# A decode-attention loop: the gather of a head's sums moved into the next pass, and half of a small projection moved ahead of the last gather

## Chip, cores and metric

The kernel runs on one core of a Trainium2 chip. The metric is the time of one execution in device microseconds (us). "Span" is the time from the first to the last instruction in the trace; it is about 1.7 us shorter than the time of the same run.

## The reference

Two independent blocks of attention for one new token, joined in the last dimension. Both have 32 query heads of 128, a query projection `x @ wq` and an output projection `@ wo` to 512 columns.

```
A: 32 heads, each with its own K and V of 32768 keys          (the large block)
B: 8 K/V heads shared by 4 query heads each, last 4096 keys   (the small block)

q = (x @ wq), per head;  p = softmax(q . K^T / sqrt(128));  o = p @ V
out = concat(o_A @ wo_A, o_B @ wo_B)                          all bf16
```

A head of the large block needs 8 MB of K and 8 MB of V. In all 570 MB have to come from HBM, and each byte is used once.

## The kernel before

The small block comes first. Then the TensorE (PE) and the VectorE (DVE) run a loop over the 32 heads of the large block; the loads are issued without a loop. The parts that matter (cuts marked with `...`, the comments are added here):

```python
        for g in range(NQH):
            self.loop = {"pe": g, "dve": g // 2}
            self.load_k(g, 1 if 0 < g < NQH - 1 else 2)   # K, the first and the last head's in two halves
            self.load_v(g)
            self.emit_qcopy(g)
            self.emit_unit("A", g)     # transpose K, score it (psT, kt, psS)
            self.emit_stats("A", g)    # maximum and exponentials
            self.emit_PT("A", g)
            self.emit_PV("A", g)       # V product (psACC), folds, gather
        self.loop = {}
        for n in ("B", "A"):
            for part in range(len(self.WO_CUTS[n]) - 1):
                self.load_wo(n, part)  # B in 2 pieces, A in 6 ever smaller ones
        self.emit_spread("A")
        self.emit_proj()               # small block's projection, then the large one's
```

The V product leaves four 4x128 blocks per strip in PSUM. The end of `emit_PV`:

```python
        pv = self.emit_gather(name, g, DH, DH + 1)      # the sum of exponentials
        ...
        for j in range(4):                              # four "folds" on the VectorE
            ...                                         # oc = block * one-hot (+ oc)
        self.accread = o
        self.gath = self.emit_gather(name, g, 0, DH)    # "gather": adds the head's row to psG
```

So at the end of each pass the TensorE waits for four folds, does one small product (the gather), goes back to the loop's top, and can then begin to transpose the next K. K sits in thirds of a buffer of which a head uses two; V has one buffer. The next K load is issued in the middle of a unit, the next V load when the V product is done.

## Time and profile before

| | before |
|---|---|
| time, median of the first 3 runs | 1323.44 us (1322.58 to 1323.79) |
| time, median of the 6 runs on record once the result was in (the same 3 and 3 more) | 1322.7 us (1322.35 to 1323.79) |
| span of the profiled run | 1321.7 us |
| distance of two 8 MB landings in the loop (K, V, K, ...) | 19.3 us throughout |
| last landing of projection weights | 1318.8 us |

First the page's slices. Each digit is the busy share of one fortieth of the span in tenths, or the TensorE clock granted in it:

```profile
PEclk9886788887878888787888878888887788888788
DMA  9999999999999999999999999999999999999998
```

The transfers are busy from end to end. The page's groups of instructions (busy time and mean ns of one, then the idle time before them and what ended most of it):

```profile
L557 DVE COPY kt<-psT 128x1024 bf16<-128x1024 bf16 x1056 | 654.3, 683 | 236.9 <-PE psT L553 235.5
L553 PE MATMUL psT<-ident,kbuf 128*128 128x128 bf16 x8448 | 577.8, 234 | 169.0 <-DMA kbuf<-in_A_k_cache_dram 154.4
```

The second line has the TensorE waiting 154.4 us for K. One boundary between passes in the timeline (start, length, engine, line and operation; in brackets the idle time before it and what ended it):

```profile
1234.97 0.33 SPq L326 DMA_DIRECT2D vbuf<-in_A_v_cache_dram  x1
...
1236.58 0.41 PE L683 MATMUL psG<-oc_A,hw 128*32 128x128 f32 x2 [1.63 <-DVE oc_A L672]
1241.26 5.15 PE L553 MATMUL psT<-ident,kbuf 128*128 128x128 bf16 x64 [4.27 <-DMA kbuf<-in_A_k_cache_dram]
```

The next V load is issued at 1234.97, the gather waits 1.63 us for the folds, and then 4.27 us pass until K has landed. So the queue always has the next load before the current one ends. Only the last boundary is different, because the last K comes in halves:

```profile
1274.41 0.41 PE L683 MATMUL psG<-oc_A,hw 128*32 128x128 f32 x2 [1.64 <-DVE oc_A L672]
...
1275.77 3.82 PE L553 MATMUL psT<-ident,kbuf 128*128 128x128 bf16 x64 [0.95 <-PEq L262]
```

Here K had landed, and 1.36 us lie between gather and transpose; 0.95 of them are put down to the TensorE's sequencer (PEq), which is the loop's back edge. The tail, from the last V product (L656) over the last gather (L683), the small block's projection (L733), the copy of its four strips (L736) and their sum (L737) to the large block's projection (L741, L719) and the store:

```profile
1284.84 2.70 SPq L326 DMA_DIRECT2D kbuf<-in_A_wo_dram  x6
...
1300.21 6.30 PE L656 MATMUL psACC<-vbuf,ptsb 128*4 128x512 bf16 x64 [0.69 <-ACT ptsb L631]
...
1308.19 0.41 PE L683 MATMUL psG<-oc_A,hw 128*32 128x128 f32 x2 [1.64 <-DVE oc_A L672]
...
1309.61 3.31 PE L733 MATMUL psS<-kbuf,oz_B 128*1 128x512 bf16 x32
...
1312.97 0.69 DVE L736 COPY pb<-psS 128x512 f32<-128x512 f32 x1 [3.07 <-PE psS L733]
...
1313.71 1.02 PE L737 MATMUL psACC<-pb,e 128*1 128x512 f32 x2 [0.80 <-DVE pb L736]
...
1314.57 2.10 PE L741 MATMUL psT<-kbuf,oz_A 128*1 128x512 bf16 x9
...
1319.09 0.93 PE L719 MATMUL psPT<-kbuf,oz_A 128*1 128x256 bf16 x14
...
1320.55 0.25 SPq L755 DMA_DIRECT2D out_dram<-out_sb  x1
```

The TensorE never waits for weights there. The last of the six loads, issued by 1287.1, took 31.7 us to land (the page's DMA issues), which gives the 1318.8 of the table.

### The profile page before, as it was taken

Reading aid. Unit: us, or ns where it says so; the run is one execution under the profiler, and the core shown is the slowest. Engines: PE = TensorE matmul, PEld = TensorE weight load, DVE = VectorE, ACT = ScalarE, POOL = GpSimd, SP = SyncE. Lnnn points to the kernel's source line nnn. Section 1 sums busy time; section 2 is a strip of 40 time slices with the busy share of each in tenths; the row PEclk is TensorE's granted clock in tenths of the full one; section 3 lists DMA queues with packets and bytes.
Section 4 is the critical chain, followed back from the end, with each engine's and each line's share of the span. In section 5 each row is a group of like instructions: output and inputs, shape, how many; then the busy total and the mean of one; then the engine's idle time right before and its main releaser. Section 6 shows DMA issues by size and latency. Waiting matters only on the chain. (4 is left out here: it accounts for less than half of the span.)

```text
span 1321.7 us, 28783 instructions
## 1 busy us (share of the span) xinstructions
PE 968.2 (73%) x13243; PEld 673.7 (51%) x13243; DVE 750.7 (57%) x1341; ACT 55.1 (4%) x168; POOL 2.6 (0%) x22
## 2 busy tenths in 40 slices
PE   4675768777677878767787777678777667877787
PEld 3353446555444655544465544446554445555453
DVE  3563556664555666455566645556665456665563
ACT  0000000000000000000000000000000000000000
POOL 0000000000000000000000000000000000000000
PEclk9886788887878888787888878888887788888788
DMA  9999999999999999999999999999999999999998
GB/s 404 434 434 431 440 434 434 434 436 432 433 436 436 428 438 434 428 438 434 428 442 430 428 442 432 430 438 434 437 432 432 438 430 434 438 428 436 436 428 365
DMA packets 13359, 570.59 MB, mean 432 GB/s; under 512 B 1570, under 2 KB 1700, under 8 KB 2084
## 3 DMA queue, kind: packets, MB, share of 16 engines
q1 hardware_dynamic: 13060, 570.43, 99.8%
q8 instruction: 8, 0.13, 0.0%
q10 hardware_dynamic: 288, 0.00, 0.0%
q14 instruction: 3, 0.02, 0.0%
HBM read 570.43 MB, written 0.00 MB: 432 GB/s over the span
## 5 line engine op out<-in xcount | busy, mean ns | idle before, releaser
L557 DVE COPY kt<-psT 128x1024 bf16<-128x1024 bf16 x1056 | 654.3, 683 | 236.9 <-PE psT L553 235.5
L553 PE MATMUL psT<-ident,kbuf 128*128 128x128 bf16 x8448 | 577.8, 234 | 169.0 <-DMA kbuf<-in_A_k_cache_dram 154.4
L553 PEld LDWEIGHTS psT<-ident,kbuf 128*128 128x128 bf16 x8448 | 538.1, 106 | 261.2 <-DMA kbuf<-in_A_k_cache_dram 162.5
L656 PE MATMUL psACC<-vbuf,ptsb 128*4 128x512 bf16 (+1 forms) x2112 | 187.0, 531 | 22.8 <-ACT ptsb L631 22.0
L576 PE MATMUL psS<-kt,qw 128*32 128x512 bf16 x2048 | 157.7, 385 | 14.9 <-DVE kt L557 14.9
L670 DVE TENSOR_SCALAR oc_A<-psACC,hot_A 128x128 f32<-128x128 f32 x32 | 11.2, 350 | 251.9 <-PE psG L683 251.9
L656 PEld LDWEIGHTS psACC<-vbuf,ptsb 128*4 128x4 bf16 (+1 forms) x2112 | 59.8, 111 | 140.4 <-issue 93.1
L604 ACT ACTIVATE psb<-psS,nb_A 128x512 bf16<-128x512 f32 x32 | 22.0, 687 | 1166.5 <-DVE nb_A L603 1166.5
L576 PEld LDWEIGHTS psS<-kt,qw 128*32 128x32 bf16 x2048 | 34.0, 95 | 57.6 <-DVE kt L557 30.8
L683 PE MATMUL psG<-oc_A,hw 128*32 128x128 f32 (+1 forms) x128 | 19.3, 227 | 52.3 <-DVE oc_A L672 52.3
L683 PEld LDWEIGHTS psG<-oc_A,hw 128*32 128x32 f32 x128 | 11.4, 109 | 62.4 <-DVE oc_A L672 55.0
L628 PE MATMUL psPT<-ident,psb 128*128 128x128 bf16 x136 | 18.3, 279 | 34.0 <-ACT psb L604 34.0
L672 DVE SCALAR_TENSOR_TENSOR oc_A<-psACC,hot_A,oc_A 128x128 f32<-128x128 f32 x96 | 33.6, 350 | 3.4
L593 DVE TENSOR_REDUCE tr_in<-psS 128x1 f32<-128x512 f32 x34 | 23.5, 692 | 17.2 <-PE psS L576 17.2
L628 PEld LDWEIGHTS psPT<-ident,psb 128*128 128x128 bf16 x136 | 10.3, 119 | 37.1 <-ACT psb L604 36.7
L597 PE MATMUL psACC<-rows,tr_in 128*1 128x64 f32 x64 | 8.7, 217 | 25.6 <-DVE tr_in L593 25.6
L631 ACT ACTIVATE ptsb<-psPT 128x512 bf16<-128x512 bf16 x34 | 20.3, 597 | 30.9 <-PE psPT L628 30.9
L597 PEld LDWEIGHTS psACC<-rows,tr_in 128*1 128x1 f32 x64 | 2.7, 81 | 35.1 <-DVE tr_in L593 35.1
L601 PE MATMUL psACC<-mr_A,nscale 1*128 1x1 f32 x64 | 12.1, 256 | 9.8 <-DVE mr_A L600 9.8
L601 PEld LDWEIGHTS psACC<-mr_A,nscale 1*128 1x128 f32 x64 | 9.4, 182 | 15.8 <-DVE mr_A L600 15.8
L603 DVE COPY nb_A<-psACC 128x1 f32<-128x1 f32 x32 | 5.0, 157 | 15.1 <-PE psACC L601 15.1
L600 DVE TENSOR_REDUCE mr_A<-psACC 1x1 f32<-1x64 f32 x32 | 6.8, 213 | 11.7 <-PE psACC L597 11.7
(82 smaller groups left out, 74.9 us busy)
## 6 DMA issues: line engine op xcount, KB each, us to landing
kbuf<-in_A_k_cache_dram SPq DMA_DIRECT2D x4, 4096.0 KB, 23.2
kbuf<-in_B_k_cache_dram SPq DMA_DIRECT2D x2, 4096.0 KB, 31.6
vbuf<-in_B_v_cache_dram SPq DMA_DIRECT2D x2, 4096.0 KB, 25.4
vbuf<-in_B_wq_dram SPq DMA_DIRECT2D x1, 4096.0 KB, 12.4
vbuf<-in_A_wq_dram SPq DMA_DIRECT2D x1, 4096.0 KB, 31.9
kbuf<-in_B_wo_dram SPq DMA_DIRECT2D x2, 2048.0 KB, 33.1
kbuf<-in_A_wo_dram SPq DMA_DIRECT2D x1, 1408.0 KB, 27.4
kbuf<-in_A_wo_dram SPq DMA_DIRECT2D x1, 1024.0 KB, 29.5
```

Source lines behind the costliest of these rows:

```text
L553: inst = e.transpose(T[:, 128 * k:128 * k + 128], src[:, DH * k:DH * k + DH], self.ident[:, :])
L557: self.copies.append(self.op("dve", lambda v: v.tensor_copy(KT[:, :], T[:, :]), o, to="pe"))
L576: inst = e.matmul(self.S[32 * c:32 * c + 32, :], lhsT=win, rhs=self.kt[(bb + c // 2) % NKT][:, 512 * (c % 2):512 * (c % 2) + 512], start=b ...
L593: o = dve(lambda v: v.reduce_max(tr["in"][:, 0:1], self.S[:, :], axis=AXX), self.sdone, self.k_pool, to="pe" if name == "A" else None)
L597: o = self.op("pe", lambda e: e.matmul(self.ACC[0:1, 0:64], lhsT=tr["in"][:, 0:1], rhs=self.rows64[:, :], start=True, stop=True, skip_grou ...
L601: o = self.op("pe", lambda e: e.matmul(self.ACC[:, 64:65], lhsT=self.nscale[:, :], rhs=t["mr"][0:1, :], start=True, stop=True, skip_group_ ...
L604: self.sread = self.op("act", lambda s: s.activation(out=self.psb[:, :], in_=self.S[:, :], func=ACTF.Exp, bias=t["nb"][:, k:k + 1], scale= ...
L628: inst = e.transpose(PT[:, 128 * jj:128 * jj + 128], self.psb[:, 128 * jj:128 * jj + 128], self.ident[:, :])
L631: self.ptread = self.op("act", lambda s: s.activation(out=self.ptsb[:, :], in_=PT[:, 0:512], func=ACTF.Copy), self.psread, to="pe")
L656: inst = e.matmul(acc[32 * c:32 * c + rows, 0:512], lhsT=lhsT, rhs=rhs, start=begin, stop=end, tile_position=(0, 32 * c), skip_group_check ...
L672: o = self.op("dve", lambda v, src=src, hot=hot: v.scalar_tensor_tensor(out=oc, in0=src, scalar=hot, in1=oc, op0=ALU.mult, op1=ALU.add), p ...
L683: return self.op("pe", lambda e: e.matmul(self.G[0:32, c0 + c:c0 + c2], lhsT=win, rhs=t["oc"][g % len(t["oc"])][:, c:c2], start=False, sto ...
```

## The change

The gather of head g-1 moves to the top of pass g, so the loop's back edge runs while the VectorE folds. A gather of zeros is added to the first pass; one more buffer is cleared for it, and the clearing of another one moves up. Behind the loop, the first 16 of the small block's 32 projection products go ahead of the last gather, into the wait for the last folds.

```diff
             self.emit_qcopy(g)
+            self.gath = self.emit_gather("A", g - 1, 0, DH)
             self.emit_unit("A", g)
...
+        self.emit_proj_b(0)
+        self.gath = self.emit_gather("A", NQH - 1, 0, DH)
         self.emit_spread("A")
         self.emit_proj()
...
+        pool(lambda g: g.memset(c["A"]["oc"][0][:, :], 0.0))
+        self.k_hw = pool(lambda g: g.memset(self.hw[:, :], 0.0))
...
         self.accread = o
-        self.gath = self.emit_gather(name, g, 0, DH)
+        if name == "B":
+            self.gath = self.emit_gather(name, g, 0, DH)
...
     def emit_proj(self):
...
-        for part in range(len(self.WO_CUTS["B"]) - 1):
-            o = self.proj_part("B", part, ...)
+        o = self.emit_proj_b(1)
```

## The prediction

> **What bounds the kernel now.** The transfers. The page's slice table shows the DMA row at 9 in every slice but the last. In the trace each 8 MB K or V load lands 19.3 us after the one before it, from the first head to the last; the output projection's pieces follow in the same stream, the last at 1318.8 us of the 1321.7 us span. The TensorE is not the limit inside the loop: in the table of groups its transposes stood idle 154.4 us for K loads, about 4.8 us a pass (4.27 us in the timeline at 1241 us). The next V load is issued at 1234.97 us, 6 us before K has landed, so the queue never runs dry.
>
> **What the change does in a pass.** The order of work on the TensorE stays. The gather waits 1.63 us for the four VectorE folds (0.35 us each); behind it comes the loop's back edge: in the timeline of the last boundary the gather starts at 1274.41, the next transpose at 1275.77, and 0.95 us of that is sequencer. Now the back edge runs inside the 1.63 us, and a transpose can start about 1.1 us sooner. In 30 passes that only lengthens the wait for K: worth 0. Added: one gather of zeros (0.4 us) and one small memset, both hidden.
>
> **Where it can count.** Only from the last head on. K's first half lands at 1270.2, before the TensorE is free, so the last unit, its statistics and its V product start about 1.0 us sooner; the last V load (landed 1299.2) then just becomes the limit. Behind it:
> - Half of the small block's projection has its weights at 1304.1, before the V product ends, so it fits into the folds' 1.64 us. Of the 3.3 us (32 products at half clock) about 1.65 us leave the chain. The loop's exit, now ahead of this half, gives part back.
> - But the other half's weights land at 1309.0 only, and the large block's pieces at 1312.3, 1314.8, 1316.7, 1317.9, 1318.5 and 1318.8. The TensorE, 2 to 2.7 us ahead, runs into these landings.
>
> Now the last landing comes 2.84 us before the end of the span. At the least, what follows it is two products (0.35), a copy (0.41) and the store with its issue (1.2): about 2.0 us. So at most 0.8 to 0.9 us can be won.
>
> **The clock.** [...] 0.50 in 1300 to 1305 us and in 1310 to 1312 us, 1.0 around them. Filling the fold wait should keep the clock up there; waiting for weights may lower it and return some tenths. It also scatters single runs (1322.58 to 1323.79 now).
>
> **Prediction:** 1322.7 us, 8 in 10 within 1322.0 to 1323.4. Faster by over 2%: 0.005; within 2%: 0.99; slower: 0.005.
>
> **What would show it.** Loads still 19.3 us apart and the last landing within 0.5 us of 1318.8; idle time for K up by 20 to 35 us in sum; the gap from gather to first transpose at the last boundary down from 1.36 to about 0.3 us; 16 products of the small projection before the last gather; new waits for projection weights; last landing to end of span 2.0 to 2.3 us.
>
> **What would make it wrong.** If the loads had gaps that I can't see, 1.1 us a pass could be real (up to 35 us). If the loop's exit cost more than the fold wait, or the clock fell in the tail, the gain would be 0 or a small loss.

## More of the kernel before

The tail's stretches, with the granted clock (PEclk) and the DMA share:

```profile
core 0: us, PE busy (x) PEld busy (x) DVE busy (x) ACT busy (x) POOL busy (x), PEclk, DMA share, GB/s
1305.00:1308.60 3.60, 1.96 (x28) 0.68 (x18) 1.40 (x4) 0.00 (x0) 0.00 (x0) 0.91 0.97 416
1308.60:1312.00 3.40, 2.60 (x28) 0.97 (x32) 0.68 (x3) 0.00 (x0) 0.00 (x0) 0.57 0.99 422
1312.00:1315.50 3.50, 2.70 (x19) 0.70 (x12) 1.37 (x2) 0.00 (x0) 0.00 (x0) 0.93 0.99 414
```

## The result

| | before | after |
|---|---|---|
| time, median (range), 6 runs each | 1322.7 us (1322.35 to 1323.79) | 1322.9 us (1322.25 to 1323.36) |
| ratio after/before, 95% interval | | 1.000 (0.9987 to 1.0013) |
| span of the profiled run | 1321.7 us | 1321.5 us |
| last landing | 1318.8 us | 1318.9 us |
| last landing to end of span | 2.84 us | 2.66 us |

A ratio is the mean time of one kernel's fast runs over that of the other's of the same rounds, so it is not quite the ratio of the medians quoted. The change is worth nothing that these runs can see.

In the loop, the slices and the groups are as before:

```profile
PEclk9777798878879888787888878788887878888798
DMA  9999999999999999999999999999999999999998
```

```profile
L557 PE MATMUL psT<-ident,kbuf 128*128 128x128 bf16 x8448 | 581.2, 235 | 164.7 <-DMA kbuf<-in_A_k_cache_dram 151.3
```

The boundary in the timeline of the changed kernel:

```profile
1234.66 0.33 SPq L326 DMA_DIRECT2D vbuf<-in_A_v_cache_dram  x1
...
1236.27 0.41 PE L688 MATMUL psG<-oc_A,hw 128*32 128x128 f32 x2 [1.64 <-DVE oc_A L676]
...
1241.32 3.91 PE L557 MATMUL psT<-ident,kbuf 128*128 128x128 bf16 x35 [4.64 <-DMA kbuf<-in_A_k_cache_dram]
```

The gather still starts right behind the folds, and the transposes still start at K's landing. The time between the two is fixed by others at both ends. The back edge has left that time, but nothing got shorter. At the last boundary, where K is there already, the back edge shows:

```profile
1274.81 0.41 PE L688 MATMUL psG<-oc_A,hw 128*32 128x128 f32 x2 [1.64 <-DVE oc_A L676]
...
1275.15 3.82 PE L557 MATMUL psT<-ident,kbuf 128*128 128x128 bf16 x64
```

1.36 us have become 0.34. The tail:

```profile
1299.55 4.72 PE L660 MATMUL psACC<-vbuf,ptsb 128*4 128x512 bf16 x64 [0.69 <-ACT ptsb L635]
...
1304.23 1.03 PE L737 MATMUL psS<-kbuf,oz_B 128*1 128x512 bf16 x16
...
1305.94 0.41 PE L688 MATMUL psG<-oc_A,hw 128*32 128x128 f32 x2 [0.68 <-DVE oc_A L676]
...
1309.08 1.88 PE L737 MATMUL psS<-kbuf,oz_B 128*1 128x512 bf16 x16 [1.85 <-DMA kbuf<-in_B_wo_dram]
...
1311.01 0.69 DVE L745 COPY pb<-psS 128x512 f32<-128x512 f32 x1 [3.55 <-PE psS L737]
...
1311.76 1.86 PE L746 MATMUL psACC<-pb,e 128*1 128x512 f32 x2 [0.80 <-DVE pb L745]
...
1313.42 3.12 PE L750 MATMUL psT<-kbuf,oz_A 128*1 128x512 bf16 x9
...
1318.95 0.93 PE L725 MATMUL psPT<-kbuf,oz_A 128*1 128x256 bf16 x14
...
1320.41 0.25 SPq L764 DMA_DIRECT2D out_dram<-out_sb  x1
```

The last gather comes 2.25 us earlier than before (1305.94 against 1308.19), although the V product started only 0.66 us earlier: it also ran partly at full clock (4.72 us in place of 6.30). Then the second 16 products of the small projection wait 1.85 us for their weights and take 1.88 us where the first 16 took 1.03. At the copy of the strips 1.96 us of the lead are still there (1311.01 against 1312.97). Behind it the strips' sum takes 1.86 us in place of 1.02 and the first nine products of the large block 3.12 in place of 2.10. By the last 14 products 0.14 us of lead is left. So the wait for weights has used up little more than the 16 products in front of the gather had saved; the lead that the earlier gather gave goes to the slower products behind. The stretches say why they are slower:

```profile
core 0: us, PE busy (x) PEld busy (x) DVE busy (x) ACT busy (x) POOL busy (x), PEclk, DMA share, GB/s
1305.00:1308.60 3.60, 0.93 (x14) 0.30 (x6) 1.50 (x6) 0.00 (x0) 0.00 (x0) 1.00 0.97 415
1308.60:1312.00 3.40, 2.12 (x17) 0.46 (x18) 0.69 (x1) 0.00 (x0) 0.00 (x0) 0.51 1.00 426
1312.00:1315.50 3.50, 3.50 (x7) 0.76 (x6) 0.68 (x1) 0.00 (x0) 0.00 (x0) 0.50 1.00 418
```

The clock is at half for practically the whole of 1308.6 to 1315.5, twice as long as before. In the clock records of these two traces the clock is full or half (1.0 or 0.5), and every record but the last, which is cut short, lasts a multiple of 3.41 us; 3.41 us are called a window below.

### The profile page after: what moved, and what is told of

Same layout as the page of the kernel before. It is cut to its first block, busy times and chain, and to the rows that moved or that the text cites. A ratio compares the mean times of both kernels' runs of the same rounds, so it can differ in the third digit from the quotient of the medians.

```text
span 1321.5 us, 28788 instructions
## 1 busy us (share of the span) xinstructions
PE 969.9 (73%) x13245; PEld 676.6 (51%) x13245; DVE 751.6 (57%) x1341; ACT 55.1 (4%) x168; POOL 2.8 (0%) x23
## 4 chain that ended last, share of the span: by engine, by line
DMA 66%; PE 27%; DVE 1%; issue 0%; ACT 0%; PEldq 0%; SPq 0%
DMA kbuf<-in_A_k_cache_dram 63%; PE psT L557 22%; PE psS L580 3%; DMA kbuf<-in_B_wo_dram 3%; DVE kt L561 1%; PE psACC L660 0%; PE psT L750 0%; PE psPT L725 0%; PE psS L737 0%; PE psACC L746 0%; PEldq L234 0%; ACT psb L608 0%; SPq L326 0%; DVE pb L745 0%; DVE tr_in L597 0%
## 5 line engine op out<-in xcount | busy, mean ns | idle before, releaser
L557 PE MATMUL psT<-ident,kbuf 128*128 128x128 bf16 x8448 | 581.2, 235 | 164.7 <-DMA kbuf<-in_A_k_cache_dram 151.3
L660 PE MATMUL psACC<-vbuf,ptsb 128*4 128x512 bf16 (+1 forms) x2112 | 182.8, 521 | 22.8 <-ACT ptsb L635 22.0
L499 PE MATMUL psACC<-vbuf,x_B 128*2 128x512 bf16 x32 | 3.6, 627 | 13.6 <-DMA x_B<-in_B_x_dram 13.6
## 6 DMA issues: line engine op xcount, KB each, us to landing
kbuf<-in_B_wo_dram SPq DMA_DIRECT2D x2, 2048.0 KB, 32.8
```

The source lines that it names most:

```text
L557: inst = e.transpose(T[:, 128 * k:128 * k + 128], src[:, DH * k:DH * k + DH], self.ident[:, :])
L660: inst = e.matmul(acc[32 * c:32 * c + rows, 0:512], lhsT=lhsT, rhs=rhs, start=begin, stop=end, tile_position=(0, 32 * c), skip_group_check ...
```

## The experiments

My theory: (1) the loop is bound by the transfers, so the saved back edge, though real, is invisible; (2) in the tail the gain runs into the landings of the projection weights, and what is left between the floor that the last landing sets and the end is a matter of the clock. The rivals: the saving does not exist even on the TensorE; or it exists and is eaten by the loop's exit and the clock alone, not by landings.

### Light loads in the loop: q_before, q_after, q_fill

To take away what the loop waits for, both kernels got lighter loads. Their outputs are wrong, which doesn't matter for the times. (Shortened; the last head's K, in two parts, is cut to a quarter in the same way.)

```diff
 load_k:   # from the fourth large head on, a quarter of each K load
-            self.load(self.kbuf[:, w * lo:w * lo + 2 * w], src, ...)
+            n = 2 * w if g < 3 else w // 2
+            self.load(self.kbuf[:, w * lo:w * lo + n], src[:, 0:n], ...)
 load_v:   # a quarter of each V load
-        self.load(self.vbuf[:, :], self.kv_src("v", "A", g)[:, 0, :], ...)
+        n = HALF * DH // 2
+        self.load(self.vbuf[:, 0:n], self.kv_src("v", "A", g)[:, 0, 0:n], ...)
```

> The kernel before, but from the fourth large head on each K load moves a quarter of its bytes, and each V load of the large block a quarter (the result is wrong on purpose). My theory: the loop stops waiting for transfers, a pass takes what the TensorE and VectorE chain needs, about 34 us in place of 38.6, so about 1150 to 1190 us in all; the idle time of transposes for K falls from 154 us to below 40. The gap between the gather and the next transpose at each back edge is 1.36 us. The rival (the saved time does not exist even on the TensorE, since the order of work is the same) expects the same of this run.

> The changed kernel with the same lighter loads. My theory: without the wait for transfers the hidden back edge shows, 0.9 to 1.2 us a pass, so 25 to 35 us less than q_before, plus 1 us or so in the tail. Rival: the gather waits for the same folds, so nothing is saved; under 3 us less than q_before.

Measured: q_before 1179.72 us, q_after 1108.62 us (medians of 4). 71 us less, twice what I expected. Who waited for whom, on the TensorE of q_before (total us, times, longest):

```profile
PE psT L556 <- PEq L262: 28.8, 31, 1.0
```

This line, the 31 back edges, is gone in q_after. The boundaries of the two kernels, q_before and then q_after:

```profile
623.49 0.41 PE L686 MATMUL psG<-oc_A,hw 128*32 128x128 f32 x2 [1.63 <-DVE oc_A L675]
...
624.81 1.40 PE L556 MATMUL psT<-ident,kbuf 128*128 128x128 bf16 x22 [0.91 <-PEq L262]
```

```profile
615.35 0.41 PE L691 MATMUL psG<-oc_A,hw 128*32 128x128 f32 x2 [1.64 <-DVE oc_A L679]
...
615.69 1.51 PE L560 MATMUL psT<-ident,kbuf 128*128 128x128 bf16 x24
```

So the saving on the TensorE is real, 1.0 us a pass, and the full loads hide it: the first rival falls. But 1.0 us times 31 is only 31 us. The mean granted clock rose from 0.871 to 0.921; as the clock is full or half in the records, the time at half clock is 2 x (1 - clock) x span, with unrounded clocks 304 us in q_before and 174 us in q_after. From the traces of the profiled runs, means over passes 3 to 31 (a whole pass is counted from V product to V product; the profiled q_before was the slowest of its four runs, 1183.32 us):

| per pass, us | q_before | q_fill | q_after |
|---|---|---|---|
| whole pass | 34.16 | 32.97 | 31.86 |
| gather to first transpose | 1.33 | 1.33 | 0.34 |
| first transpose to the reduction of the scores | 20.95 | 20.39 | 20.38 |
| V product | 6.14 | 5.59 | 5.55 |
| time at half clock in the whole run | 304 | 208 | 174 |

The clock as the cause of the rest was tested by itself in q_fill. It is q_before with four idle products in the fold wait of each pass, and it shortens no chain:

```diff
         self.accread = o
+        if name == "A":
+            self.fill_pe(4)     # 4 products of 512 columns into an unused PSUM row
         self.gath = self.emit_gather(name, g, 0, DH)
```

> q_before (light K and V loads, back edge where it was), plus four idle products of 512 columns on the TensorE in each pass, while it waits for the folds (0.9 us at full clock, 1.7 at half, so inside the wait or hardly over it). Question: q_after was 71 us faster than q_before, of which the trace gives 1.0 us a pass (31 us) to the back edge. Theory: the other 1.3 us a pass is the clock, which a shorter idle stretch keeps up; then this run, which shortens no chain, is 25 to 45 us faster than q_before, its half-clock time falls from 304 us to 170 to 220 us, and the gap from gather to transpose stays 1.33 us. Rival: the rest comes from the moved order itself; then q_fill is within 5 us of q_before or slower.

Measured: 1146.47 us, 33 us less than q_before's median (that ran on another chip; the ratios to the kernel before of their own rounds are 0.8668 and 0.8918). The four idle products took 1.03 us a pass (32.8 us in 32). More work on the TensorE made the kernel faster. The back edge stayed at 1.33 us, and units and V products took the times that they have in q_after. So of the 71 us, about 31 are the back edge and about 33 the clock that the idle products keep up; some 7 are left that no run separates.

### Light weights in the tail: w_before, w_after

Here K and V are loaded in full, and each load of projection weights moves a quarter of its bytes (wrong results again).

```diff
 load_wo:
-        self.load(self.kbuf[:, off + 512 * a0:off + 512 * a1], src[:, 512 * a0:512 * a1], ...)
+        self.load(self.kbuf[:, off + 512 * a0:off + 384 * a0 + 128 * a1],
+                  src[:, 512 * a0:384 * a0 + 128 * a1], ...)
```

> The kernel before, with full K and V loads, but each load of output projection weights moves a quarter of its bytes (wrong result on purpose). Its last landing moves from 1318.8 to about 1304 us. My theory: the kernel before does not wait for these weights, so its time stays within 1 us of the kernel before (1322.7). Rival (before is bound by the last landing itself): 2 us or more faster.

> The changed kernel with the same lighter weight loads. My theory (the tail's gain is swallowed by waits for the weights' landings): with the landings gone the end comes 3 to 5.5 us before that of w_before. Rival (the gain was never there: the loop's exit and the half clock ate it): under 1.5 us before that of w_before.

Measured: w_before 1323.31 us (1321.95 to 1323.69), w_after 1320.01 us (1319.87 to 1320.78). With the last landing at 1304.9 and 1304.7, the kernel before gains nothing by its median, and the changed kernel ends 3.3 us sooner by the medians (2.9 by the means, just under the 3 to 5.5 that I expected). The small projection in w_before, and its second half in w_after:

```profile
1309.61 1.90 PE L733 MATMUL psS<-kbuf,oz_B 128*1 128x512 bf16 x32
```

```profile
1308.49 1.03 PE L737 MATMUL psS<-kbuf,oz_B 128*1 128x512 bf16 x16
```

Neither waits for weights. So the tail's gain exists on the TensorE. Its size needs care, because the clock differs too: both profiled runs had full clock in the tail from 1305.3 us or earlier (the strips' sum took 1.02 us and the first nine products of the large block 2.10 in each), and with that their spans are 1320.3 and 1318.3, 2.0 us apart. The other three runs of w_before, not profiled, took 1.3 to 1.7 us longer than its profiled one. For the same reason these two runs do not yet decide between landings and clock; `fill` below does.

Nor is the kernel before held by the last landing in most of its runs: three of the four w_before runs took as long as it does, or longer. Only the profiled one, 1321.95 us at full clock, ended below the fastest time of the kernel before in the same rounds (1322.33). So at full clock the landings seem to hold it too; `b_fill` below tests that.

### What is left in the tail: move_only, fill, fine

The kernels from here on give correct results.

`move_only` is the changed kernel with the first half of the small projection put back behind the gather and the spread:

```diff
-        self.emit_proj_b(0)
         self.gath = self.emit_gather("A", NQH - 1, 0, DH)
...
     def emit_proj(self):
+        self.emit_proj_b(0)
         o = self.emit_proj_b(1)
```

> The changed kernel with the first half of the small projection put back behind the last gather and the spread (the gather stays in the next pass). Theory: the TensorE waits for the second half's weights (1309.0) anyway, the first half then fills that wait; the time is that of the changed kernel within its scatter, 1322.4 to 1323.1, last landing to end 2.1 to 2.9 us. Rival (the half ahead of the gather is worth its 1.65 us): 1 us or more slower than the changed kernel.

Measured: 1322.61 us (1322.38 to 1323.23), ratio to before 0.9997 (0.9983 to 1.0010); last landing to end 2.00 us in its profiled run, a little under the 2.1 that I had named as least. In its trace the 32 products run from 1308.52 without a wait, since the other half's weights land (1308.9) while the first half runs. So the half in front of the gather buys nothing in time.

`fill` is the changed kernel with idle products in the tail's waits:

```diff
         self.emit_proj_b(0)
+        self.fill_pe(2)
         self.gath = self.emit_gather("A", NQH - 1, 0, DH)
+        self.fill_pe(2)
         self.emit_spread("A")
...
     def emit_proj(self):
+        self.fill_pe(8)
         o = self.emit_proj_b(1)
+        self.fill_pe(3)
```

> The changed kernel with idle products in the tail's waits (2 behind the first half, 2 behind the last gather, 8 before and 3 behind the second half), to keep the clock up. Theory: the half clock in the tail takes the rest of the gain; with full clock from about 1309 us to the end the TensorE meets every landing of the large block's weights, and last landing to end falls from 2.65 us to 2.0 to 2.2 us; the runs come closer together, 1322.1 to 1322.6. Rival (products after the last landing set the end whatever the clock was before): stays 2.5 us or more, time as the changed kernel.

Measured: 1322.60 us (1322.42 to 1322.66), ratio 0.9996 (0.9982 to 1.0009). Five runs within 0.24 us, while the kernel before spread over 1.5 us in the same rounds (1322.32 to 1323.8). Stretches and last steps of its tail:

```profile
1308.60:1312.00 3.40, 3.24 (x27) 1.03 (x25) 0.69 (x1) 0.00 (x0) 0.00 (x0) 1.00 1.00 423
1312.00:1315.50 3.50, 3.50 (x28) 1.69 (x27) 1.17 (x2) 0.00 (x0) 0.00 (x0) 1.00 1.00 420
```

```profile
1316.62 0.82 PE L727 MATMUL psPT<-kbuf,oz_A 128*1 128x256 bf16 x12 [0.77 <-DMA kbuf<-in_A_wo_dram]
...
1318.81 0.08 PEld L727 LDWEIGHTS psPT<-kbuf,oz_A 128*1 128x1 bf16 x2 [0.25 <-DMA kbuf<-in_A_wo_dram]
1319.11 0.41 DVE L734 CAST out_sb<-psPT 1x256 bf16<-1x256 f32 x1 [3.42 <-PE psPT L727]
...
1319.61 0.25 SPq L778 DMA_DIRECT2D out_dram<-out_sb  x1
```

At full clock the TensorE waits for the large block's pieces, the weights of the last two products go in 0.05 us behind the last landing (1318.76), and the span ends 1.97 us behind it. This is the floor. It also settles the second rival: fill and w_after both had full clock behind the gather, and their spans are 1320.7 with the landings and 1318.3 without, so at full clock the landings take 2.4 us. The changed kernel's profiled run, with half clock there, had a span of 1321.5, another 0.8 us.

`fine` loads the second half of the small block's weights in three pieces (8, 4 and 4 rows), so that only 4 products wait for the last of them:

```diff
-    WO_CUTS = {"A": (0, 11, 19, 25, 29, 31, 32), "B": (0, 16, 32)}
+    WO_CUTS = {"A": (0, 11, 19, 25, 29, 31, 32), "B": (0, 16, 24, 28, 32)}
```

> The changed kernel with the second half of the small block's weights loaded in three pieces (8, 4 and 4 rows), so that only 4 products wait for 1309.0 us. Theory: the small projection ends 0.5 to 1.3 us sooner, but the large block's first landing at 1312.3 is the next limit and the clock may fall in the wait: last landing to end 2.0 to 2.7 us, time within 0.6 us of the changed kernel. Rival (the small block's last landing is what holds the end): faster by about as much as the small projection ends sooner.

Measured: 1322.90 us (1322.67 to 1323.28), ratio 0.9998 (0.9984 to 1.0012). The small projection ended at 1309.5 in place of 1311.0, but the clock was at half again (0.5 from 1309.4 to 1316.2; the strips' sum took 1.87 us and the first nine products of the large block 3.95), and the end came 2.47 us behind the last landing. Less waiting at one place does not help while the next landing is at 1312.4.

### The order of before, with the clock kept up: b_fill and after_again

`b_fill` is the kernel before with the four idle products of q_fill in each pass, two behind the loop's exit and three ahead of the strips' sum. `after_again` is the changed kernel unedited.

```diff
         self.accread = o
+        if name == "A":
+            self.fill_pe(4)
         self.gath = self.emit_gather(name, g, 0, DH)
...
+        self.fill_pe(2)
         self.emit_spread("A")
...
+        self.fill_pe(3)
         strips = self.op("dve", ...)
```

> The kernel before, order unchanged, plus idle products in its waits: four in each pass while the folds run, two behind the loop's exit, three ahead of the strips' sum. Theory: the scatter of the kernel before (1322.3 to 1323.8) is the clock in its tail, and its lucky runs already end at the floor that the last landing sets; with the clock kept up its runs lie within 1322.2 to 1322.8, as those of fill do, without the moved gather. Loads stay 19.3 us apart, half-clock time falls by 50 us or more without any effect on the loop. Rival (the moved gather is needed to reach the floor, or more TensorE work costs time): 1323.0 or more.

> The changed kernel again, unedited, on the same chip and in the same rounds as b_fill. Theory: 1322.2 to 1323.4 with a scatter of 0.7 us or more, mean within 0.5 us of the kernel before; b_fill scatters less than half as much.

Measured, b_fill: 1322.67 us median, ratio 1.000 (0.9987 to 1.0014), three runs at 1322.62 to 1322.67, but two outside of what I expected, 1323.03 and 1324.0. Their spans are 1321.1 and 1320.9, so the 1324.0 at least lost its time outside of the span. By device times b_fill thus scattered as much as after_again (1.4 and 1.1 us), and what I had put, less than half, failed; it holds for the spans only, which I looked at afterwards. All five spans lie within 1320.9 to 1321.1; those of after_again (1323.45 us median, 1322.47 to 1323.55) reach from 1320.8 to 1321.9, in two groups, and those of the kernel before from 1320.6 to 1323.5. The profiled b_fill ends 1.96 us behind its last landing, with the clock at 1.00 from 1308.6 to 1315.5. So the kernel before reaches the same floor when its clock stays up, without the moved gather. The time at half clock fell by 48 us (clock 0.836 to 0.854), a little less than the 50 that I had written, and the loop did not move: a pass took 38.46 us on average in both, the shorter last one included.

| profiled run | last landing to end, us | clock at half behind the last V product |
|---|---|---|
| before | 2.84 | 1309.1 to 1312.5 |
| after, after_again | 2.66, 2.84 | 1308.6 to 1315.5, 1309.7 to 1316.6 |
| fine | 2.47 | 1309.4 to 1316.2 |
| move_only | 2.00 | 1308.2 to 1311.6 |
| fill, b_fill | 1.97, 1.96 | none |

The clock is not all of it. The runs of before and move_only had the same 3.4 us of half clock (one window), but move_only's last gather came 0.91 us earlier (1307.28 against 1308.19), and it ended at the floor. So in a run with one such window the moved gather can be worth 0.84 us. The two profiled runs of the change had two windows at half clock, and lost it. This is one pair of traces, not a test.

## Why the prediction was right

The time was right: 1322.7 predicted, 1322.9 measured, within the range and within 2%. That the loop would give nothing was understood; that the number came out so close was partly luck, since the 0.74 us of gain in it did not come and the 1323.44 that it was taken from was a high median of three runs. Point by point:

- **The loop is bound by transfers, and the back edge is worth 0 there.** Right. Landings stayed 19.3 us apart, and with light loads the same edit showed its 1.0 us a pass.
- **"Idle time for K up by 20 to 35 us in sum."** Wrong, and it is the clearest error: 154.4 us became 151.3. The step that failed is "a transpose can start about 1.1 us sooner. In 30 passes that only lengthens the wait for K". The wait in the trace runs from the gather to the landing. The gather's start is set by the folds and did not move, and the back edge had been inside that idle time all along. The time saved was never counted apart from the wait, so it could not be added to it.
- **The gap at the last boundary.** 1.36 to about 0.3 us predicted, 0.34 measured.
- **The V product about 1.0 us sooner.** 0.66 measured (1300.21 to 1299.55), as the pass before it ended 0.4 us later in this run. "The last V load then just becomes the limit" holds in fill and w_after, where that landing ends the V product's wait (1.36 and 1.19 us idle); in the profiled run it started 0.27 us behind it.
- **"The loop's exit ... gives part back."** Wrong: from the sum's gather at 1304.11 to the first projection product at 1304.23 there is nothing to see. The back edge costs its 0.95 us, leaving the loop did not.
- **The TensorE runs into the landings.** Right: 1.85 us of wait for the small block's second half. What all the landings together cost, fill and w_after show: 2.4 us of span at full clock.
- **Last landing to end 2.0 to 2.3 us.** The floor of about 2.0 was right (1.96 to 2.00 in move_only, fill and b_fill); the profiled run of the change had 2.66. I had named the falling clock only as a risk of "some tenths". It was not rare: both profiled runs of the change had it, and of its eleven runs six lie at 1323.2 to 1323.6 and five at 1322.2 to 1322.6.
- **A gain of 0.74 us against the 1323.44 of then.** Not there. That median came from three runs; three more made it 1322.7. The kernel before in its lucky runs (1322.35) takes as long as fill and b_fill at the floor (1322.42 to 1322.67 in most runs), so the only thing left to win was its scatter, and that the change did not remove.

## What to carry to other kernels

Ask of each saved wait which event ends the next one: where both ends of an idle stretch are set by others, here folds and a landing, work taken out of it is worth nothing, and the idle time does not even grow. In a kernel bound by transfers, compute the floor first (last landing plus what must follow it), and compare the fastest run with it before expecting a gain. And where a kernel is bound by the TensorE in bursts, idle products in its waits can be worth as much as a shorter chain, because they hold the clock: 33 us of 1180 in the runs with light loads (mean granted clock 0.909 with them, 0.871 without). With full loads the same products in b_fill gained nothing in the loop.

## What the traces show of the clock and the back edge

- **Short gaps and the clock.** In the tail of the changed kernel no gap of the TensorE was longer than 1.85 us, and the clock fell (0.5 from 1308.6 us). In the trace of before, sorted by the 3.41 us windows of the clock records (the first begins at 25.7 us), each of the 68 full windows after which the clock fell had the TensorE's products busy for at most 50% of it, and no full window over 50% was followed by half (in fine one at 51% was); four full windows at 48 to 50% stayed full. Each of the 67 half windows after which it rose was busy for 79% or more; the 60 that stayed at half were busy for 79% at most. These are the shares of one trace.
- **Transposes.** In the trace of before, units made of transposes with some scoring products between them ran at full clock: 1.00 over all of 1271.6 to 1298.8 us. 32 of its half-clock windows held nothing but transposes of K on the TensorE and were followed by a full one (for example 121.25 to 124.66 us at 0.50, busy throughout, then 1.00 to 128.07); 23 more, busy for 74% at most, stayed at half.
- **The scatter of whole runs.** Spans reached from 1320.6 to 1322.1 us in nine runs of the kernel before, and from 1320.7 to 1321.0 in five of fill, whose waits were filled, in the same rounds. What else sets the runs of one kernel apart, no run here shows.
- **The back edge.** The back edge of this loop, which also resets its semaphores, cost 0.93 us of TensorE idle time each in q_before (28.8 us in 31). Which part of it is the branch, no run separates.
